# Seven-product hidden layer: a ScalarE copy from PSUM bank to PSUM bank that later products add onto, and ScalarE copies where VectorE added

## The chip, the cores and the metric

The kernel runs on one core of a Trainium2 chip. The engines are named as in the profile: PE is TensorE's matmul and PEld its weight load, DVE is VectorE, ACT is ScalarE, POOL is GpSimd, SP is the engine that issues most DMAs. PE writes its results to PSUM banks (128 partitions x 512 float32), and DVE and ACT read them from there. The metric is the device time of one execution in microseconds, as the median of several runs; lower is better.

## The reference

Two blocks follow each other, all in float32. `x` is (8, 8, 512, 64): batch, head, token, depth; `state` is (8, 8, 32, 64).

```python
scores  = scale * x @ state^T;   a  = softmax(scores);   xread = a @ state
scores2 = scale * state @ x^T;   a2 = softmax(scores2);  sread = a2 @ x
t = concatenate([xread, sread], axis=2)        # (8, 8, 544, 64)
t = t.transpose(0, 2, 1, 3).reshape(8 * 544, 512)
h = t @ w_in                                   # (4352, 2048)
g = h * erf(softplus(h))
out = g @ w_out                                # (4352, 512)
```

## The kernel before

Each batch gives 512 token rows and 32 state rows. Batch 0 runs through a start of its own, whose order of steps is written out in a long string. Batches 1 to 7 run through one loop with two **rounds** per batch, 14 in all; a round makes one half of the 2048 hidden columns for the 512 token rows of its batch. The state rows of all batches come last (`hidden_states`, `project7`).

A round calls `hidden_wide`. The product of the attention weights `aT` (512 tokens) and the mixed weights `m` is cut into 2 x 2 blocks, and the four blocks c11, c12, c21, c22 of the hidden layer are made with seven block products in place of eight (the Winograd form of Strassen's scheme). The sums of blocks that go in stand in `sx` and `sy`, made earlier on DVE by `combine_m` and `combine_a`. `hidden_wide` goes through two **halves** (`o` = 0 and 1), and each half makes the seven products for two blocks of 128 hidden columns, so there are 28 halves. `product(n, bank, first)` is two matmuls of float32, which PE runs in two passes each: four passes and four weight loads of L489. With `first` false the product is added onto what the bank holds.

A half of before uses two banks of `ps_h` (tile `h`), then two of `ps_at` (tile `at`); both pools have two buffers. The scheme's sums are taken so: with P1 to P7 the products,

- product 1 goes to bank p, ACT copies it to `m1` in SBUF (L495);
- product 6 goes to bank q, DVE makes u2 = m1 + P6 (L499 by way of L472);
- product 2 is added onto P1 in p, ACT copies c11 (L504);
- product 7 is added onto P6 in q, DVE makes u3 = m1 + P6 + P7 (L508);
- product 5 in a new bank, DVE makes c22 = u3 + P5 (L514); product 4 in another, DVE makes c21 = u3 + P4 (L517);
- product 3 is added onto P5, DVE makes c12 = u2 + P5 + P3 (L522).

All five adds go through the helper `add`, so the profile puts them at L472. u2 and u3 lie in the places of c12 and c21 in the SBUF tile `ring`. ACT takes Softplus of each block (L482), in the order 0, 3, 2, 1; the last one of a half (`late`) is emitted in the next half, or at the end. The first Softplus of a round stands behind an ACT table load.

Between the products stand two kinds of other work. `between()` takes one **piece** of the projection of the round before (`project_wide`, two matmuls of L641; in the first round one 512 wide matmul of L926), with the copies and adds that follow from it (L646, L664 on ACT, L626 on DVE; in the first round the copy L932 on ACT). `fill(budget)` takes DVE steps from a list: softmax steps of the next batch, transposes, `combine_m`, differences of `w_out`. Instructions on PE, DVE and ACT run in the order in which they are emitted:

```python
in_order(begun, [nc.tensor, nc.vector, nc.scalar])
```

After `hidden_wide` a round takes erf on ACT, multiplies by the hidden block on DVE (L1127), makes sums of blocks (L673, L674), and projects with seven products again (`project_wide`), during which attention scores, `mixed_pair` (L383 to L386) and reads for the next batches are woven in.

Of the kernel before, what the change touches and what calls it, by code (L numbers as in the profile page):

```python
# [9 lines left out]
F32 = mybir.dt.float32  # L10
# [7 lines left out]
def kernel(  # L18
# [17 lines left out]
    nc = tc.nc  # L36
    B, H, S, D = x.shape
    Ns = state.shape[2]
    d_model, d_ff = moe_w_in.shape
    P = 128  # L40
# [19 lines left out]
    ps_at = ctx.enter_context(tc.tile_pool(name="ps_at", bufs=2, space=PSUM))  # L60
# [408 lines left out]
    def hidden_wide(b, g, low, between, fill, later):  # L469

        bank = lambda: ps_h.tile([P, S], F32, name="h")
        add = lambda o, x, y: nc.vector.tensor_tensor(o, x, y, op=ALU.add)  # L472
        view = lambda t: t.rearrange("p (h u) -> p h u", h=2)
        late = None
        for o in range(2):
            s, hs = ([ring[:, u, low:low + 2, k, 2 * o:2 * o + 2].rearrange(
                "p h i t -> p h (i t)") for k in range(4)] for u in range(2))
            c11, c12, c21, c22 = hs
            m1, u2, u3 = s[3], c12, c21

            def softplus(k, s=s, hs=hs):
                nc.scalar.activation(out=s[k], in_=hs[k], func=ACTF.Softplus)  # L482

            def product(n, bank, first=True):
                x, y = X[b, g][n - 1], Ys[b][n - 1]
                out = bank.rearrange("p (h i t) -> p i h t", h=2, i=2)
                for i in range(2):
                    q = P * (2 * o + i)
                    nc.tensor.matmul(out=out[:, i], lhsT=x[:, q:q + P], rhs=y,  # L489
                                     start=(first and i == 0), stop=(i == 1),  # L490
                                     skip_group_check=not first)

            p, q = bank(), bank()
            product(1, p)
            nc.scalar.copy(m1, view(p))  # L495
            if late:
                late(1)
            product(6, q)
            add(u2, m1, view(q))  # L499
            if o or not later:  # L500
                between()
            fill(1.8)
            product(2, p, False)
            nc.scalar.copy(c11, view(p))  # L504
            if not o and later:
                between()
            product(7, q, False)
            add(u3, m1, view(q))  # L508
            softplus(0)
            between()  # L510
            fill(1.2)
            p, q = (ps_at.tile([P, S], F32, name="at") for _ in range(2))
            product(5, p)
            add(c22, u3, view(p))  # L514
            product(4, q)
            softplus(3)
            add(c21, u3, view(q))  # L517
            between()
            fill(0.6 if o else 1.2)
            product(3, p, False)  # L520
            softplus(2)
            add(c12, u2, view(p))  # L522
            fill(0 if o else 1.2)
            late = softplus
        late(1)
# [551 lines left out]
    for n, name in enumerate(steps0):  # L1077
        if n == len(steps0) - 40:
            overlap = traced()
        n, _, name = name.rpartition("*")  # L1080
# [17 lines left out]
    def fill(budget):  # L1098
        while jobs and jobs[0][0] <= budget + 0.01:
            cost, f = jobs.popleft()  # L1100
            budget -= cost
            f()
# [32 lines left out]
    for n, (b, u) in enumerate((b, u) for b in range(1, B) for u in range(2)):  # L1135
# [42 lines left out]

        steps = pending()
        hidden_wide(b, o, low, lambda: next(steps, None), fill, n == 0)  # L1180
        erf_part(inner, outside)
        for k, _ in enumerate(steps):
# [141 lines left out]
```

## Time and profile before

| | before |
|---|---|
| time, median of 3 runs | 716.93 us (716.89 to 716.95) |
| profiled execution, span from first to last instruction | 716.0 us |
| PE busy, TensorE matmul instructions in the trace | 709.2 us (99%), 4291 |
| DVE busy | 541.9 us (76%), 880 instructions |
| ACT busy | 378.9 us (53%), 535 instructions |
| DVE adds of L472, from `at` and from `h` | 84 x 680 ns, 56 x 679 ns |
| ACT copies L495 and L504 | 28 x 585 ns, 28 x 586 ns |
| ACT Softplus L482 and its table loads | 112 x 631 ns, 14 x 1283 ns |

The span runs from the first to the last instruction of one profiled execution; the device time of a run also has what lies around it. Busy times of the engines overlap. PE's ends are modelled, so that a busy PE may still have short gaps; the distance between the starts of its passes or of its weight loads is the better measure. "Idle before" and the name behind the arrow say how long an engine stood before an instruction and what released it.

### The profile page before, as it was taken

What the parts mean: (1) busy time and instruction counts of PE and PEld (TensorE: products, weight loads), DVE (VectorE), ACT (ScalarE), POOL (GpSimd) and SP (SyncE); (2) the same over time, 40 slices, a digit from 0 to 9 for tenths busy, and PEclk for the clock granted to TensorE, in tenths of its full rate; (3) what the DMA queues carried; (4) which work ended last, traced back from release to release, by engine and by line L of the source; (5) the groups of instructions that cost most, each with busy time, mean ns of one, the idle gap of its engine ahead of it and who ended that gap; (6) DMA issues with size and microseconds to landing.
All of it is one profiled execution on the core that took longest, in us unless ns stands there. A gap on an engine that the chain in (4) does not pass through costs nothing.

```text
span 716.0 us, 10962 instructions
## 1 busy us (share of the span) xinstructions
PE 709.2 (99%) x4291; PEld 562.4 (79%) x4291; DVE 541.9 (76%) x880; ACT 378.9 (53%) x535; POOL 25.2 (4%) x34
## 2 busy tenths in 40 slices
PE   8999999999999999999999999999999999999998
PEld 6444347688878878887888878887888888889997
DVE  6997888889868987698776877697777757665533
ACT  4999895647364526544455445562464535442340
POOL 0000000000100000000000000000000000000000
PEclk9999999999999999999999999999999999999999
DMA  8779686750358162514523280615242322002100
GB/s 257 236 209 251 210 243 180 169 159 31 52 98 205 28 140 40 161 37 106 80 41 138 58 148 1 177 31 144 34 120 70 95 41 27 33 29 30 25 7 30
DMA packets 144068, 74.65 MB, mean 104 GB/s; under 512 B 123024, under 2 KB 132624, under 8 KB 142480
## 3 DMA queue, kind: packets, MB, share of 16 engines
q1 hardware_dynamic: 139152, 65.89, 33.8%
q0 software_dynamic: 4032, 7.34, 7.6%
q8 instruction: 34, 0.56, 0.3%
q10 hardware_dynamic: 832, 0.72, 0.3%
q14 instruction: 18, 0.15, 0.1%
HBM read 49.81 MB, written 20.45 MB: 98 GB/s over the span
## 4 chain that ended last, share of the span: by engine, by line
PE 97%; DMA 2%; ACT 0%; SPq 0%; DVE 0%; issue 0%
PE o L641 48%; PE h L489 14%; PE at L489 10%; PE o L926 8%; PE h L534 3%; PE o L616 3%; PE at L919 2%; PE h L919 2%; PE h L383 2%; DMA raw<-in_moe_w_out_dram 2%; PE at L383 2%; PE at L275 1%; PE o L224 1%; DMA x<-in_x_dram 1%; PE at L908 1%; PE at L1018 0%
## 5 line engine op out<-in xcount | busy, mean ns | idle before, releaser
L641 PE MATMUL o<-w_out,ring 128*128 128x256 f32 x896 | 203.0, 379 | 0.0
L641 PEld LDWEIGHTS o<-w_out,ring 128*128 128x128 f32 x896 | 169.8, 190 | 24.9 <-DVE ring L1127 0.8
L641 PE MATMUL o<-raw,ring 128*128 128x256 f32 x672 | 161.4, 381 | 0.0
L641 PEld LDWEIGHTS o<-raw,ring 128*128 128x128 f32 x672 | 126.5, 190 | 25.9 <-ACT m L385 9.2
L482 ACT ACTIVATE ring<-ring 128x512 f32<-128x512 f32 x112 | 70.6, 631 | 59.8 <-DVE ring L472 59.2
L489 PE MATMUL h<-aT,m 128*128 128x256 f32 x336 | 81.9, 379 | 0.0
L1127 DVE TENSOR_TENSOR ring<-ring 128x1024 f32<-128x1024 f32 (+1 forms) x61 | 70.7, 1201 | 4.5 <-ACT ring L546 4.5
L489 PEld LDWEIGHTS h<-aT,m 128*128 128x128 f32 x336 | 63.8, 190 | 10.2 <-issue 0.9
L472 DVE TENSOR_TENSOR ring<-ring,at 128x512 f32<-128x512 f32 x84 | 57.2, 680 | 16.9 <-PE at L489 15.2
L926 PE MATMUL o<-w_out,ring 128*128 128x512 f32 x128 | 59.5, 599 | 0.0
L626 DVE TENSOR_TENSOR ot<-uv,o 128x256 f32<-128x256 f32 (+1 forms) x56 | 31.0, 553 | 30.1 <-PE o L641 28.1
L472 DVE TENSOR_TENSOR ring<-ring,h 128x512 f32<-128x512 f32 x56 | 38.0, 679 | 20.0 <-PE h L489 19.9
L664 ACT COPY ot<-o 128x256 f32<-128x256 f32 x28 | 10.4, 372 | 77.9 <-PE o L641 77.9
L704 POOL DMA_DIRECT2D out_dram<-ot x28 | 24.5, 946 | 652.1 <-DVE ot L626 574.8
L926 PEld LDWEIGHTS o<-w_out,ring 128*128 128x128 f32 x128 | 23.7, 190 | 28.1 <-issue 26.6
L626 DVE TENSOR_TENSOR ot<-ot,o 128x256 f32<-128x256 f32 x56 | 22.2, 417 | 27.9 <-ACT ot L664 27.7
L504 ACT COPY ring<-h 128x512 f32<-128x512 f32 x28 | 16.4, 586 | 47.9 <-PE h L489 47.9
L673 DVE TENSOR_TENSOR ring<-ring 128x512 f32<-128x512 f32 x56 | 38.6, 689 | 1.4
L674 DVE TENSOR_TENSOR ring<-ring 128x512 f32<-128x512 f32 x56 | 36.3, 685 | 0.0
L385 ACT COPY m<-h 128x512 f32<-128x512 f32 x13 | 7.6, 586 | 46.7 <-PE h L383 46.6
L546 ACT ACTIVATE ring<-ring 128x2048 f32<-128x2048 f32 x16 | 30.5, 1904 | 0.0
L489 PE MATMUL at<-sy,sx 128*128 128x256 f32 x112 | 28.7, 379 | 0.0
(203 smaller groups left out, 965.8 us busy)
## 6 DMA issues: line engine op xcount, KB each, us to landing
w_in<-kept_in SPq DMA_DIRECT2D x7, 2048.0 KB, 8.2
out_dram<-ot SPq DMA_DIRECT2D x33, 256.0 KB, 2.2
raw<-in_moe_w_in_dram SPq DMA_DIRECT2D x16, 512.0 KB, 5.4
raw<-in_moe_w_out_dram SPq DMA_DIRECT2D x8, 1024.0 KB, 5.9
xq<-in_x_dram SPq DMA_DIRECT2D x112, 64.0 KB, 3.2
x<-in_x_dram SPq DMA_DIRECT2D x56, 128.0 KB, 3.0
out_dram<-ot POOLq DMA_DIRECT2D x28, 256.0 KB, 4.5
sc<-xT SPq DMA_DIRECT2D x112, 32.0 KB, 1.9
```

What stands on the lines that cost most here:

```text
L383: nc.tensor.matmul(out=ps[k][e][q, :], lhsT=st[r, b, q], rhs=of_group[g][r, :, i, :], start=True, stop=True)
L472: add = lambda o, x, y: nc.vector.tensor_tensor(o, x, y, op=ALU.add)
L482: nc.scalar.activation(out=s[k], in_=hs[k], func=ACTF.Softplus)
L489: nc.tensor.matmul(out=out[:, i], lhsT=x[:, q:q + P], rhs=y, start=(first and i == 0), stop=(i == 1), skip_group_check=not first)
L546: nc.scalar.activation(out=s, in_=s, func=ACTF.Erf)
L626: add = lambda o, x, y: tt(o, x, y, op=ALU.add)
L641: nc.tensor.matmul(out=out, lhsT=lhs[:, i, :], rhs=rhs[:, g, i, :], start=(start and i == 0), stop=(i == GF - 1), skip_group_check=not start)
L673: return [lambda: tt(S1, A21, A22, op=ALU.add), lambda: tt(S2, S1, A11, op=ALU.subtract), lambda: tt(S3, A11, A21, op=ALU.subtract), lambd ...
L674: lambda: tt(S3, A11, A21, op=ALU.subtract), lambda: tt(S4, A12, S2, op=ALU.subtract)]
L919: nc.tensor.matmul(out=h_t[g, i], lhsT=m_t[0, g][:, e, P * i:P * i + P], rhs=aT[0][:, e], start=start, stop=not start)
L926: nc.tensor.matmul(out=acc[r], lhsT=gT[g][:, i, P * r:P * r + P], rhs=w_out[:, GF * g + i, :], start=(made_of[r] == 1), stop=(made_of[r] = ...
L1127: nc.vector.tensor_tensor(s[:, ks], s[:, ks], hs[:, ks], op=ALU.mult)
```

## The change

In each half, ACT no longer copies product 1 to `m1` in SBUF; it copies the whole bank p into the second bank q. Product 5 moves up to stand right behind product 1, in a bank r of `ps_at`. Products 6, 7 and 4 are then all added onto the contents of q, one after the other, and after each of them ACT copies the bank out: u2, u3 and c21. The DVE adds that made u2, u3 and c21 are gone; c22 = u3 + r and c12 = u2 + r stay on DVE, and product 3 is added onto product 5 in r. A half allocates three banks in place of four. `m1` is no longer used here. The pieces, the `fill` calls and the Softplus calls stay where they were among products 6, 2, 7, 4 and 3.

```diff
-            m1, u2, u3 = s[3], c12, c21
+            u2, u3 = c12, c21
...
             p, q = bank(), bank()
+            r = ps_at.tile([P, S], F32, name="at")
             product(1, p)
-            nc.scalar.copy(m1, view(p))
+            nc.scalar.copy(q, p)
             if late:
                 late(1)
-            product(6, q)
-            add(u2, m1, view(q))
+            product(5, r)
+            product(6, q, False)
+            nc.scalar.copy(u2, view(q))
             if o or not later:
                 between()
             fill(1.8)
...
             if not o and later:
                 between()
             product(7, q, False)
-            add(u3, m1, view(q))
+            nc.scalar.copy(u3, view(q))
+            add(c22, u3, view(r))
             softplus(0)
             between()
             fill(1.2)
-            p, q = (ps_at.tile([P, S], F32, name="at") for _ in range(2))
-            product(5, p)
-            add(c22, u3, view(p))
-            product(4, q)
+            product(4, q, False)
             softplus(3)
-            add(c21, u3, view(q))
+            nc.scalar.copy(c21, view(q))
             between()
             fill(0.6 if o else 1.2)
-            product(3, p, False)
+            product(3, r, False)
             softplus(2)
-            add(c12, u2, view(p))
+            add(c12, u2, view(r))
             fill(0 if o else 1.2)
             late = softplus
         late(1)
```

In the changed kernel the ACT copies have the lines L496 (bank to bank), L501 (u2), L506 (c11), L510 (u3) and L517 (c21).

## The prediction

> **What bounds the kernel now.** I read the page first: busy time by engine, and the chain of work that ended last.
>
> ```profile
> PE 709.2 (99%) x4291; PEld 562.4 (79%) x4291; DVE 541.9 (76%) x880; ACT 378.9 (53%) x535; POOL 25.2 (4%) x34
> PE 97%; DMA 2%; ACT 0%; SPq 0%; DVE 0%; issue 0%
> ```
>
> TensorE is busy all the time and is 97% of the chain. DVE and ACT appear there with 0%: taking work off DVE pays only where PE waits for DVE, and putting work on ACT costs only where PE comes to wait for ACT. The fourteen rounds (calls of `hidden_wide`, two halves each) that the change touches lie between 107 and 633 us. Second view, busy time by stage (after the stage: its length, PE busy, PEld busy, DVE, ACT), and third, what the weight loads waited for in that stage (total, times, longest).
>
> ```profile
> 100.00:640.00 540.00, 540.00 (x3248) 448.24 (x3247) 423.30 (x707) 274.61 (x407) 21.08 (x24) 1.00 0.39 90
> PEld h L489 <- DVE ring L472: 0.3, 1, 0.3
> PEld h L489 <- ACT ring L495: 0.3, 1, 0.3
> ```
>
> PE is busy for all 540 us at clock 1.00, and of 784 weight loads of L489 one waited for a DVE add (L472) and one for the ACT copy (L495). So the DVE adds cost no time now. The fourth view is the order of time in one round (start, duration; x4 means four weight loads, one product), weight loads first, then ACT:
>
> ```profile
> 459.64 0.84 PEld L489 LDWEIGHTS h<-aT,m 128*128 128x128 f32 x4
> 460.50 0.84 PEld L489 LDWEIGHTS h<-sy,sx 128*128 128x128 f32 x4
> 461.36 0.84 PEld L641 LDWEIGHTS o<-w_out,ring 128*128 128x128 f32 x4
> ...
> 468.27 0.84 PEld L489 LDWEIGHTS h<-aT,m 128*128 128x128 f32 x4
> 460.92 0.59 ACT L495 COPY ring<-h 128x512 f32<-128x512 f32 x1 [0.49 <-PE h L489]
> 463.51 0.59 ACT L504 COPY ring<-h 128x512 f32<-128x512 f32 x1 [2.00 <-PE h L489]
> 464.11 1.28 ACT L482 ACT_TABLE_LOAD   x1
> 465.41 0.63 ACT L482 ACTIVATE ring<-ring 128x512 f32<-128x512 f32 x1
> 465.94 0.35 ACT L646 COPY uv<-o 128x256 f32<-128x256 f32 x1
> 469.55 0.59 ACT L495 COPY ring<-h 128x512 f32<-128x512 f32 x1 [1.16 <-PE h L489]
> 472.14 0.59 ACT L504 COPY ring<-h 128x512 f32<-128x512 f32 x1 [1.47 <-PE h L489]
> 472.76 0.63 ACT L482 ACTIVATE ring<-ring 128x512 f32<-128x512 f32 x1
> ```
>
> From 459.64 to 468.27 there are ten groups (seven products, three pieces of the projection), so a group takes 0.863 us and its four PE passes 0.216 each. An ACT copy of a product starts 0.42 after the next group's first weight load (460.50 to 460.92, 469.13 to 469.55).
>
> The fifth view is the one place where PE did wait for such a copy, the first half of the first round (second column: duration):
>
> ```profile
> 108.24 0.84 PEld L489 LDWEIGHTS h<-sy,sx 128*128 128x128 f32 x4
> 108.46 1.03 PE L489 MATMUL h<-sy,sx 128*128 128x256 f32 x4
> 108.72 0.57 ACT L495 COPY ring<-h 128x512 f32<-128x512 f32 x1
> 109.34 0.51 PEld L489 LDWEIGHTS h<-aT,m 128*128 128x128 f32 x3 [0.25 <-ACT ring L495]
> 110.31 1.02 PE L926 MATMUL o<-w_out,ring 128*128 128x512 f32 x2
> ```
>
> The copy ends at 109.29, the weight load starts 0.05 later, and that is 0.24 after its turn (108.24 + 0.863 = 109.10). But PE itself lost only 0.125: from 108.46 to 110.31 are 1.85 us for eight passes that take 1.725. The weight load runs ahead of its pass, and this lead hides 0.11 of a late start.
>
> **The change, part by part.** The order of the built kernel on PE is now, per half (28 of them): product 1, 5, 6, piece, 2, 7, piece, 4, piece, 3. In the very first half the first piece stands behind product 2.
>
> *What goes.* The m1 copy (L495, 585 ns) becomes the copy from bank to bank, so 28 for 28. Three of five DVE adds per half go: 84 x 0.68 = 57 us of DVE. On the path this is worth nothing, by the third view.
>
> *What comes on ACT.* Three copies of 586 ns per half, 84 x 0.586 = 49 us. A half has 5.45 us of ACT work (five copies, four Softplus) in 8.63; it fits as a mean, and what counts are the waits.
>
> *Wait 1, product 6 for the bank copy.* Only product 5 lies between product 1 and product 6: 0.863 us of cover. Needed are 0.42 + 0.586 + 0.05 = 1.056. The weight load is 0.193 late, the lead hides 0.11, PE loses 0.083. No row of before shows ACT writing into a bank. Bounds: Softplus (SBUF to SBUF) takes 631 ns, reads of a bank 586 to 597; so 631 above, which makes the loss 0.128; below, the saving on the other side too, or more, until at 503 ns nothing is lost. I take 586, the nearest row, which has one of the two ends in a bank. The Trainium skill (ScalarE: Activation LUTs, "Step-by-step: what each stage is for") says that ScalarE writes faster to PSUM than to SBUF, without a figure; no run here shows it, and by it the term would lie between 0 and 0.083. The skill also speaks against the whole edit (PSUM — Partial Sum Buffer, "Summary: rules for kernel authors"): a seed that ACT writes has to be 0, because whether the next matmul adds to it hangs on bits that ACT does not set; no row here shows such bits, and time would be the same either way.
>
> *Wait 2, product 4 for the u3 copy.* Before, product 4 had a fresh bank. Now it adds onto the bank that u3 is copied from, one group after product 7: again 0.863 of cover against 1.056, and this copy has the form of L504. PE loses 0.083.
>
> *Waits that are covered.* Product 7 waits for the u2 copy, which ends 1.87 after product 6 begins; product 7 begins 2.59 after, so 0.7 is to spare (also behind the late Softplus that the second half puts in between). Product 2 is behind product 6 and finds the copy done. Product 3 waits for c22 = u3 + r: 0.03 + 0.68 + 0.05 after the u3 copy, 2.63 after product 7 begins, against 3.54. DVE now stands still at c22 until the u3 copy is there; queued behind are the softmax, transpose and sx steps of `fill`, and c12. With three adds less per half they come no later than now, and their readers are a stage away.
>
> *ACT's queue in front of the second bank copy.* In the first half of a round the table load now stands behind the u3 copy, and behind it, in order: Softplus 0, L646, Softplus 3, the c21 copy, Softplus 2, and then the bank copy of the second half. From the end of the u3 copy, by the starts above: 0.01 + 1.30 (load) + 0.53 + 0.25 (L646 less its overlap) + 0.53 + 0.62 (a Softplus that needs the copy in front, 472.14 to 472.76) + 0.53 = 3.77. The u3 copy ends 1.87 after product 7 begins, so ACT is free at 5.64; product 1 of the second half begins at 5 x 0.863 + 0.083 = 4.40 and can be copied at 5.68. It just fits, with 0.04 to spare. In the first round L932 (604 ns) stands there in place of L646, some 0.25 longer: 0.2 us lost once. The skill (same page, "What ACT_TABLE_LOAD costs") counts 2.66 us for a table switch, load and drain. Here the Softplus starts 1.30 after the load does, so the row has no drain; by the page the bank copy would be 1.34 late in 14 rounds and the sum 18 us higher.
>
> *Sum.* Two waits in 28 halves are 56; one (fifth view) is paid already. 55 x 0.083 = 4.6, and 0.2 makes 4.8. PE has nothing to make it up with. The profiled execution has a span of 716.0 and the median is 716.93, 0.9 for what lies around it: 716.9 + 4.8 = 721.7.
>
> **Rivals.** *A, ACT's queue becomes the bound.* If the seven steps in front of the second bank copy take 0.3 longer than I add up (c22 late from DVE holds Softplus 3 and all behind it), each round loses 0.3 and more: 14 x 0.3 = 4 on top, 726 and beyond. For it: 0.04 of slack. Against: c22 has 1.3 us before Softplus 3 needs it, and DVE has less to do.
> *B, not slower: the lead of the weight load hides both waits.* Place: the first weight loads of products 6 and 4; price 0.083 each; it decides from a lead of 0.19 on. Time 717.0. For it: the lead of 0.11 is from one wait only. Against: that wait was just such a copy.
> *C, faster.* DVE with 57 us less feeds something earlier. The most there is to win in this stage is PE's gap at changes of shape, well under 5 us, and the waits put to DVE are parts of a microsecond: 716.
>
> **How the numbers follow.** Forecast 0.82, A 0.09, B 0.06, C 0.03. Below, a bank copy of 503 ns or less leaves 4.8 - 2.3 = 2.5, 719.4; above, 631 ns adds 28 x 0.045 = 1.3, and a queue 0.15 late in 13 rounds 2.0: 725.0. The range is 719.2 to 725.0; it leaves out A's worse half and B and C. What a measurement can tell from no change is 0.2%, 1.4 us; the forecast is slower in all its range, as is A: 0.91. B is the same: 0.06; C faster: 0.03.
>
> **What would show it.** After: the weight loads of L489 wait for L496 and for L510 some 28 times each, about 0.2 each; ten groups take 8.80 in place of 8.63; L496 takes 586 ns give or take 45; ACT is busy some 428 us, DVE some 485; PE still leads the chain. The forecast is wrong if those waits are absent (B), if L496 starts more than 0.1 after ACT could have had product 1 in second halves (A), or if PE's weight loads come to wait for DVE's c22 at product 3.

## The result, and the profile after

The changed kernel takes 722.12 us (median, 721.6 to 722.54) against 716.94 for the kernel before; the ratio is 1.0068, 95% interval 1.0054 to 1.0083. Both were run again beside each other on the chip of the last experiments: 722.44 against 717.72, 4.7 us apart, ratio 1.0065 (1.0052 to 1.0077). In all runs of the experiments the kernel before lies near 717.7 with spans near 716.0, so 1.8 us lie outside the span there, where the first table had 0.9. Times below are compared within one chip.

The page of the profiled execution after (722.54 us, span 720.8), busy time and chain:

```profile
PE 714.0 (99%) x4291; PEld 558.4 (77%) x4291; DVE 489.0 (68%) x796; ACT 420.9 (58%) x619; POOL 25.2 (3%) x34
PE 97%; DMA 2%; ACT 0%; issue 0%; SPq 0%; DVE 0%
```

DVE has 53 us less and ACT 42 us more, and the same PE work takes 5 us longer. The chain still puts all of it down to PE. What PE lost shows in the waits of its weight loads between 100 and 645 us (total, times, longest):

```profile
PEld h L489 <- ACT ring L510: 6.8, 28, 0.6
PEld h L489 <- ACT h L496: 6.0, 28, 0.3
```

Two waits per half, 28 times each: product 4 for the u3 copy, product 6 for the copy from bank to bank. In order of time, the weight loads of a half that answers to the one shown of before, then ACT up to the second bank copy:

```profile
462.44 0.84 PEld L489 LDWEIGHTS h<-aT,m 128*128 128x128 f32 x4
463.30 0.84 PEld L489 LDWEIGHTS at<-sy,sx 128*128 128x128 f32 x4
464.39 0.73 PEld L489 LDWEIGHTS h<-sy,sx 128*128 128x128 f32 x4 [0.25 <-ACT h L496]
465.15 0.84 PEld L641 LDWEIGHTS o<-w_out,ring 128*128 128x128 f32 x4
...
467.74 0.84 PEld L641 LDWEIGHTS o<-w_out,ring 128*128 128x128 f32 x4
468.79 0.73 PEld L489 LDWEIGHTS h<-sy,m 128*128 128x128 f32 x4 [0.21 <-ACT ring L510]
469.54 0.84 PEld L641 LDWEIGHTS o<-raw,ring 128*128 128x128 f32 x4
...
471.27 0.84 PEld L489 LDWEIGHTS h<-aT,m 128*128 128x128 f32 x4
463.77 0.57 ACT L496 COPY h<-h 128x512 f32<-128x512 f32 x1 [0.55 <-PE h L489]
468.15 0.58 ACT L510 COPY ring<-h 128x512 f32<-128x512 f32 x1 [0.28 <-PE h L489]
468.75 1.28 ACT L482 ACT_TABLE_LOAD   x1
470.05 0.63 ACT L482 ACTIVATE ring<-ring 128x512 f32<-128x512 f32 x1
470.58 0.35 ACT L646 COPY uv<-o 128x256 f32<-128x256 f32 x1
470.84 0.63 ACT L482 ACTIVATE ring<-ring 128x512 f32<-128x512 f32 x1
471.37 0.57 ACT L517 COPY ring<-h 128x512 f32<-128x512 f32 x1
471.97 0.63 ACT L482 ACTIVATE ring<-ring 128x512 f32<-128x512 f32 x1
472.55 0.57 ACT L496 COPY h<-h 128x512 f32<-128x512 f32 x1
```

Product 6's weight load starts 0.05 after the bank copy's end (463.77 + 0.57 = 464.34, 464.39), 0.23 after its turn; product 4's 0.06 after L510's end, 0.19 after its turn. The half takes 8.83 us (462.44 to 471.27) where it took 8.63. Taking each distance between the starts of PE's passes less what the pass takes without a stall (0.216 us for 256 columns, 0.429 for 512), products 6 lost 2.30 us in all and products 4 2.23: 4.53, against 0.12 before.

### The profile page after: what moved, and what is told of

The parts are those of the page before. It is cut to its first block, busy times and chain, and to the rows that moved or that the text cites. A ratio compares the mean times of both kernels' runs of the same rounds, so it can differ in the third digit from the quotient of the medians.

```text
span 720.8 us, 10926 instructions
## 1 busy us (share of the span) xinstructions
PE 714.0 (99%) x4291; PEld 558.4 (77%) x4291; DVE 489.0 (68%) x796; ACT 420.9 (58%) x619; POOL 25.2 (3%) x34
## 4 chain that ended last, share of the span: by engine, by line
PE 97%; DMA 2%; ACT 0%; issue 0%; SPq 0%; DVE 0%
PE o L641 47%; PE h L489 17%; PE o L926 8%; PE at L489 7%; PE h L534 3%; PE o L616 3%; PE at L919 2%; PE h L919 2%; PE h L383 2%; DMA raw<-in_moe_w_out_dram 2%; PE at L383 2%; PE at L275 1%; PE o L224 1%; PE at L908 1%; DMA x<-in_x_dram 1%; PE at L1018 0%
## 5 line engine op out<-in xcount | busy, mean ns | idle before, releaser
L472 DVE TENSOR_TENSOR ring<-ring,at 128x512 f32<-128x512 f32 x56 | 38.2, 682 | 86.6 <-ACT ring L510 79.5
L489 PE MATMUL h<-aT,m 128*128 128x256 f32 x336 | 81.8, 379 | 0.0
L489 PEld LDWEIGHTS h<-aT,m 128*128 128x128 f32 x336 | 63.8, 190 | 10.0 <-issue 1.2
L626 DVE TENSOR_TENSOR ot<-uv,o 128x256 f32<-128x256 f32 (+1 forms) x56 | 31.0, 553 | 37.7 <-PE o L641 35.9
L626 DVE TENSOR_TENSOR ot<-ot,o 128x256 f32<-128x256 f32 x56 | 22.1, 416 | 27.8 <-ACT ot L664 27.7
L506 ACT COPY ring<-h 128x512 f32<-128x512 f32 x28 | 16.4, 585 | 29.6 <-PE h L489 29.6
L501 ACT COPY ring<-h 128x512 f32<-128x512 f32 x28 | 16.4, 586 | 28.0 <-PE h L489 25.5
L489 PE MATMUL h<-sy,m 128*128 128x256 f32 x112 | 31.0, 399 | 0.0
L489 PE MATMUL h<-sy,sx 128*128 128x256 f32 x112 | 30.9, 398 | 0.0
```

Source lines behind the costliest of these rows:

```text
L489: nc.tensor.matmul(out=out[:, i], lhsT=x[:, q:q + P], rhs=y, start=(first and i == 0), stop=(i == 1), skip_group_check=not first)
L626: add = lambda o, x, y: tt(o, x, y, op=ALU.add)
```

## The experiments

Every kernel below was timed beside the kernel before on its chip (717.68, 717.76 and 717.72 in the three sets of runs), and times are compared by their distance to it; the change stands 4.7 above. "PE's loss" is the sum just described, for the products of L489 unless another line is named. "Cover" below is the PE work that lies between a product and the next one that needs its bank. All of them:

| run | time | ratio to before (95%) | PE's loss: product 6 / product 4 / elsewhere |
|---|---|---|---|
| the change, again | 722.44 | 1.0052 to 1.0077 | 2.29 / 2.25 / - |
| third piece before product 4 | 721.40 | 1.0042 to 1.0067 | 3.22 / 0 / - |
| first piece before product 6 | 723.89 | 1.0075 to 1.0106 | 0.13 / 2.25 / product 7: 3.55 |
| product 5 late | 744.29 | 1.0357 to 1.0386 | 26.4 / 0 / - |
| u3 copied by VectorE | 727.26 | 1.0121 to 1.0149 | 2.23 / 7.17 / - |
| product 4 in its own bank | 720.50 | 1.0029 to 1.0054 | 2.99 / 0 / - |
| both waits covered | 720.61 | 1.0029 to 1.0054 | 0.13 / 0 / projection: 2.3 more |
| the same, c22 behind fill | 717.63 | 0.9992 to 1.001 | 0.13 / 0 / - |
| order alone, c22 behind fill | 722.48 | 1.0053 to 1.0081 | 0 / 0 / product 3: 5.55 |
| order alone, c22 first | 717.29 | 0.9987 to 1.0005 | 0 / 0 / - |
| third piece before 4, Softplus 2 later | 721.09 | 1.0036 to 1.0061 | 3.00 / 0 / - |

**Is the change's cost the same on one chip?**

> The changed kernel as it is, beside the kernel before on the same chip. The traces put the stalls at 4.3 us; the kernel before took 717.7 in the runs of the experiments, 0.8 more than in the first table, all of it outside the span. Theory: 717.7 + 4.4 = 722.1 on one chip. Rival (something outside the stalls adds 0.8): 722.9.

Measured: 722.44 against 717.72. The spans are 720.7 and 716.0, so all 4.7 us lie inside them. 4.4 are the stalls (4.54 less the 0.12 of before). Some 0.3 us more lie behind PE's last pass (3.98 us from its start to the end, 3.65 in the traces of before and of the covered kernel); why is open.

**Product 5 late: the law of the wait, with nothing between.**

```diff
             product(1, p)
             nc.scalar.copy(q, p)
-            product(5, r)
             product(6, q, False)
...
             between()
             fill(1.2)
+            product(5, r)
+            add(c22, u3, view(r))
             product(4, q, False)
```

> Product 5 stands behind the second piece again, in front of product 4, so nothing lies between product 1 and product 6, and product 4 has two groups of cover. Theory: product 6 waits 0.42 + 0.571 + 0.05 - 0.11 = 0.93 us each time, 28 x 0.93 = 26.0, in place of 2.1; the wait of product 4 goes, -2.2: 722.1 + 23.9 - 2.2 = 743.8. Rival (added ScalarE work): unchanged, 722.

Measured: 744.29, and the waits of product 6 alone rise to the foreseen size:

```profile
PEld h L489 <- ACT h L496: 30.2, 28, 1.1
```

ScalarE does the same work as in the change. What changed is 0.863 us of cover per half, and PE lost 26.4 us where 26.0 were worked out; product 4, with two groups of cover now, lost nothing. The rival that ScalarE's added work is the cost falls here.

**u3 copied by VectorE: a lighter ScalarE, a slower kernel.**

```diff
-            nc.scalar.copy(u3, view(q))
+            nc.vector.tensor_copy(u3, view(q))
```

> The copy of u3 goes from ScalarE to VectorE, nothing else. Theory: what counts is how long the copy keeps the bank. VectorE starts 0.49 us after the next group's first weight load and its operations on 128x512 take about 0.68: 0.49 + 0.68 + 0.05 - 0.863 - 0.11 = 0.25 in place of 0.08 at product 4, 28 x 0.17 = 4.7 more: 726.8. Rival (added ScalarE work): ScalarE has 16 us less, the loss shrinks by about a third, 720.4. Second rival (VectorE standing still at c22 until ScalarE has copied u3 costs time): gone here, faster than 722.1.

Measured: 727.26, 9.5 above before, so 4.8 more than the change (4.7 foreseen). The group of the copy (28 x 692 ns) and the wait:

```profile
L510 DVE COPY ring<-h 128x512 f32<-128x512 f32 x28 | 19.4, 692 | 64.1 <-PE h L489 62.2 <-issue 1.8
PEld h L489 <- DVE ring L510: 11.8, 28, 0.8
```

ScalarE had 16 us less to do and PE lost 4.9 us more. What counts is how long the copy keeps the bank: 692 ns and a start 0.485 us after product 7's last pass begins, against 585 ns and 0.416. Both rivals fall.

**Undoing one wait, in two ways.** First by cover, then by a bank of its own:

```diff
+            between()
             product(4, q, False)
             softplus(3)
             nc.scalar.copy(c21, view(q))
-            between()
```

> The third piece of the projection stands in front of product 4 in place of behind it, so the u3 copy has two groups of cover (1.73 us) in place of one. Theory (each bank that ACT copies has to be free before the next product, and only what the cover leaves open costs): the wait of product 4 for L510 goes, 28 x 0.080 = 2.2 us, 722.1 becomes 719.9; the wait of product 6 for L496 stays at 0.08 each. Rival (ScalarE's 42 us of added work is what slows the kernel): that work is unchanged, so 722.1.

```diff
-            r = ps_at.tile([P, S], F32, name="at")
+            r, r4 = (ps_at.tile([P, S], F32, name="at") for _ in range(2))
+            if o:
+                r, r4 = r4, r
...
-            product(4, q, False)
+            product(4, r4)
             softplus(3)
-            nc.scalar.copy(c21, view(q))
+            add(c21, u3, view(r4))
```

> Of the changed kernel only product 4 is undone: it goes into a bank of its own and VectorE adds c21 = u3 + that bank. Theory: product 4 no longer waits for L510, 2.2 us won, 719.9, as with the third piece moved in front of it; the wait of product 6 stays. Rival (added ScalarE work): 16 of 42 us gone, 720.4, which a time alone does not tell from the theory; the weight loads' waits do.

Measured: 721.40 and 720.50. In both the wait for L510 is gone, 2.25 us of PE's loss. But the wait for the bank copy (L496, in the second run L498) grew:

```profile
PEld h L489 <- ACT h L496: 7.0, 28, 0.5
PEld h L489 <- ACT h L498: 6.7, 28, 0.3
```

PE's loss there went from 2.29 to 3.22 and 2.99, which I had not foreseen; so the first stands 3.7 above before and the second 2.7, where 2.5 was expected of both (4.7 less 2.2). The rest of the two distances, some 0.3 more and 0.4 less, is behind PE's last pass (4.26 and 3.65 us from its start to the end, 3.98 in the change). ACT's queue in the first of the two, at the second half's bank copy:

```profile
193.55 0.63 ACT L482 ACTIVATE ring<-ring 128x512 f32<-128x512 f32 x1
194.09 0.58 ACT L496 COPY h<-h 128x512 f32<-128x512 f32 x1
```

No idle time stands before L496: it follows Softplus 2 at once, 0.046 later than PE's result would have let it (1.33 after product 1's first weight load in place of 1.28). The 0.04 us to spare that the prediction had counted are used up, because product 1 now comes 0.08 earlier and the table load does not. In the first round the copy is 0.27 late. The next run tests this.

**Softplus 2 moved out of that queue.** In addition to the third piece before product 4:

```diff
             if late:
+                late(2)
                 late(1)
...
-            softplus(2)
+            if o:
+                softplus(2)
```

> The third piece in front of product 4, as in the first run, and of a first half the Softplus 2 moved behind the bank copy of the second half. Theory: the first run took away the wait of product 4 but the wait of product 6 grew from 2.2 to 2.9 us, because ScalarE's queue (table load and all behind it) has only 0.04 us to spare in front of the second bank copy and product 1 came 0.08 earlier. With 0.6 us less in that queue the growth goes: 721.4 becomes 720.7, and L496 starts 1.28 after product 1 begins in second halves. Rival (a wait of another kind): stays at 721.4.

Measured: 721.09, and product 6 lost 3.00, not the 2.3 that it loses in the change. A miss, and an instructive one:

```profile
194.09 0.57 ACT L496 COPY h<-h 128x512 f32<-128x512 f32 x1 [0.58 <-PE h L489]
```

ScalarE now stood idle for 0.58 us before the copy, so the queue no longer holds it. Yet the copy ends as late after the pass as it did: it starts 0.471 us after product 1's last pass begins and takes 570 ns, where in the first run it started after 0.461 and took 579. With no Softplus in between that waits for the c21 copy, the bank copy itself has to wait for two semaphores, PE's and ScalarE's own (the c21 copy has to have left the bank). An extra semaphore instruction then stands in front of it on ACT's queue; of L496, first in the run before, then in this one:

```profile
L496 ACTq EVENT_SEMAPHORE  x12: 17/17/862, 107.2 to 581.4; - x12
L496 ACTq EVENT_SEMAPHORE  x26: 17/17/861, 107.4 to 627.4; - x26
```

Where this extra instruction is the one that waits for PE, the copy starts 0.471 after the pass; copies with one semaphore start 0.416 after it. Where it waits for a DVE result that has long been there, as in four first halves of the change, the copy starts 0.416 after the pass all the same. The 0.471 shows in the change itself, in six of its first halves, in the run with product 4's own bank (second halves) and, below, at L503. What this run did win of PE's loss, 0.22 us, is in the first round, where the second bank copy now starts 0.471 after the pass and not 0.685.

**More cover for product 6: the wait moves.**

```diff
             product(5, r)
+            if o or not later:
+                between()
             product(6, q, False)
             nc.scalar.copy(u2, view(q))
-            if o or not later:
-                between()
```

> The first piece stands in front of product 6 in place of behind it (not in the very first half). Theory: the bank copy is covered now, 28 x 0.08 = 2.1 us won, but between products 6 and 7 only product 2 is left, 0.863 us against the 1.05 that the u2 copy needs: the same wait comes back at product 7 for L501, 0.08 each. Time 722.1, and the weight loads wait for L501 in place of L496. Rival (the bank to bank copy is what is slow): 720.0.

Measured: 723.89, 6.2 above before, 1.5 more than the change.

```profile
PEld h L489 <- ACT ring L503: 7.2, 27, 0.3
PEld h L489 <- ACT ring L510: 6.9, 28, 0.6
```

The wait left L496 and came back at product 7 for the u2 copy (L503), as foreseen. It is larger, 3.55 in 27 halves or 0.13 each, since L503 waits for two semaphores and starts 0.46 to 0.47 after the pass. The rival, that the copy into a bank is the slow thing, falls.

**Both waits covered, with the copies kept on ScalarE.**

```diff
             product(5, r)
+            if o or not later:
+                between()
             product(6, q, False)
             nc.scalar.copy(u2, view(q))
-            if o or not later:
-                between()
...
             product(2, p, False)
             nc.scalar.copy(c11, view(p))
-            if not o and later:
-                between()
+            between()
             product(7, q, False)
             nc.scalar.copy(u3, view(q))
             add(c22, u3, view(r))
             softplus(0)
-            between()
+            if not o and later:
+                between()
             fill(1.2)
-            product(4, q, False)
+            product(4, r4)
             softplus(3)
-            nc.scalar.copy(c21, view(q))
+            add(c21, u3, view(r4))
```

> Product 4 goes into a bank of its own again and c21 is a VectorE add again; the first piece stands in front of product 6 and the second in front of product 7 (not in the very first half). The bank copy and the copies of u2 and u3 stay on ScalarE. Order of a half: 1, 5, piece, 6, 2, piece, 7, 4, piece, 3. Theory: every wait has two groups of cover, so all 4.4 us of stalls go: 717 to 718, the time of before. Rival (added ScalarE work): a third of the 42 us is gone, so a third of the loss, 720.4.

Measured: 720.61, a miss. All waits of L489 for ScalarE's copies are gone (but the one of the very first half), and a new one came in the projection (L628 is the projection's add, L626 before):

```profile
PEld o L643 <- DVE uv L628: 3.0, 5, 0.6
```

The cause was looked for on VectorE, in the order of time of that kernel:

```profile
191.63 0.69 DVE L472 TENSOR_TENSOR ring<-ring,at 128x512 f32<-128x512 f32 x1 [4.05 <-ACT ring L511]
```

VectorE stands still for 4.05 us at c22, until ScalarE has copied u3, which is a group later in this order; the `fill` steps queued behind come late, and with them the projection's add. The next run moves c22 behind them and nothing else. (`r4` is a bank of its own for product 4, made as above.)

```diff
             nc.scalar.copy(u3, view(q))
-            add(c22, u3, view(r))
             softplus(0)
...
             fill(1.2)
+            add(c22, u3, view(r))
             product(4, r4)
```

> The kernel in which both waits have two groups of cover (product 4 in its own bank, c21 on VectorE, pieces in front of 6 and 7) lost its ScalarE waits but lost 0.34 us in eight rounds at the projection's add of L628 instead. Here c22 is emitted behind the fill steps, not in front of them, nothing else. Theory: VectorE stood at c22 until ScalarE had copied u3 (some 7.1 us into a half) and came late to all that was queued behind; with the fill steps in front it works in that time, the projection's waits go, 2.3 to 2.9 us, and the time is that of before on the same chip, 717.7. Rival (the bank copies on ScalarE cost something beside the waits): stays at 720.6.

Measured: 717.63, ratio 1.0001 (0.9992 to 1.001): the time of before. The five waits for L628 are gone (five in the trace, not the eight rounds of the expectation). The stay at c22 is shorter now, with work in front of it:

```profile
190.59 1.48 DVE L472 TENSOR_TENSOR ring<-ring,at 128x512 f32<-128x512 f32 x2 [2.72 <-ACT ring L511]
```

This kernel's page shows what the added work on ScalarE and the relief of VectorE are worth when no wait is left over:

```profile
PE 709.0 (99%) x4291; PEld 561.7 (78%) x4291; DVE 507.3 (71%) x824; ACT 407.9 (57%) x591; POOL 25.2 (4%) x34
```

29 us more on ACT and 35 less on DVE than before, with the copy from bank to bank kept, change the time neither way.

**The order of the products alone.** The kernel before with product 5 moved up and nothing else; c22 once behind the `fill` steps, once right behind u3.

> The kernel before with product 5 moved up behind product 1, as in the change; m1, the three VectorE adds and four banks stay as before. Theory: the order alone costs nothing, 716.9. Rival (the new order of the products, and c22 placed earlier on VectorE, costs something): up to 722.

Measured: 722.48, which at first sight spoke for the rival. But the wait named its own cause:

```profile
PEld at L489 <- DVE ring L472: 9.1, 20, 0.8
```

In my edit c22 had stayed behind the `fill` steps, and with product 5 in front product 7 comes one group later, so that product 3 found its bank not yet read. Hence the second run:

> The kernel before with only product 5 moved up (all five VectorE adds, m1 and four banks as before), and c22 right behind u3 on VectorE as in the change, where the run before it had c22 behind the fill steps and product 3 waited for it, 5.5 us in all. Theory: that wait was the place of c22; product 3 finds its bank free, and the time falls from 722.5 to 717.7 or, if VectorE with its full load then comes late to the steps behind, to 718 to 720. Rival (the new order itself costs): stays near 722.5.

Measured: 717.29, ratio 0.9996 (0.9987 to 1.0005). The order is free. Placing c22 behind `fill` is a loss with five adds on VectorE and a gain with three: the same line, judged by what stands idle.

No version beat the kernel before beyond the noise. The trace of before has PE busy for all of 540 us in these rounds. By the starts of its passes the projection, the largest part of that, loses 1.5 us in 15 gaps of 0.10; what the smaller parts lose was not worked out.

## Why the prediction was right

The forecast was 721.7, in a range of 719.2 to 725.0; measured 722.1. Term by term:

- *The mechanism* is as forecast: the copy keeps the bank longer than one group covers. Undone alone, doubled in cover, lengthened (VectorE) and left bare (product 5 late) the waits answered by the sum 0.42 + copy + 0.05 - cover - 0.11, within 0.5 us over 28 halves; what it left out is the second semaphore, 0.04 to 0.055 where it counts.
- *Wait 1* was put at 0.083; it is 0.063 in most halves, 0.118 in the six whose copy starts 0.471 after the pass, 0.082 on the mean. That the mean came out is luck: a copy that is 15 ns shorter than assumed and a second semaphore that was not foreseen cancel. The copy into a bank takes 571 ns, not 586. The Trainium skill (ScalarE: Activation LUTs, "Step-by-step: what each stage is for") has ScalarE faster towards PSUM; here that is 14 ns against the same copy into SBUF (L510, 585 ns).
- *Wait 2* was put at 0.083; it is 0.080.
- *The lead of 0.11*, read from one wait, held: from it 0.93 and 0.25 were worked out for two of the experiments, and 0.94 and 0.26 came.
- *ACT's queue* was put at 3.77 us and its slack at 0.04. In the trace shown, the u3 copy ends at 468.73 and Softplus 2 starts at 471.97; a copy behind a Softplus can start 0.54 after it (193.55 to 194.09 above), so ScalarE was free 3.78 after the u3 copy, and the bank copy started 0.04 later. Rival A was as close as that, and the third piece before product 4 tipped it.
- *The first round* was put at 0.2 for L932; PE lost 0.06 there, since the copy started 0.04 late and took 595 ns. This term was mis-sized: it puts L932 in the place of L646, in front of Softplus 3, but the trace has it behind the c21 copy:

```profile
116.45 0.57 ACT L517 COPY ring<-h 128x512 f32<-128x512 f32 x1
116.91 0.59 ACT L932 COPY ot<-o 128x512 f32<-128x512 f32 x1
117.39 0.64 ACT L482 ACTIVATE ring<-ring 128x512 f32<-128x512 f32 x1
117.92 0.59 ACT L496 COPY h<-h 128x512 f32<-128x512 f32 x1
```

  There it fills part of the time in which Softplus 2 waits for the c21 copy. From L517 to Softplus 2 are 0.94 us, where the round shown above takes 0.60 (471.37 to 471.97): 0.34 longer, of which L646 had taken 0.26 in its own place (470.58 to 470.84). With the third piece in front of product 4, L932 does stand in front of Softplus 3, and the copy is the 0.27 late named above.
- *The table load*: 468.75 to 470.05 is 1.30 again, as in the row of before. The Trainium skill (ScalarE: Activation LUTs, "What ACT_TABLE_LOAD costs") counts 2.66 with a drain; no run here shows a drain behind these loads.
- *DVE's relief is worth nothing*: shown by the covered kernel. *DVE standing at c22* was called harmless, which is right for the change (L626's waits did not grow) but has little room: one group later it cost 2.3 us.
- *The other signs* came: the half shown takes 8.83 us against 8.80. ACT is busy 420.9 us against 428 and DVE 489.0 against 485, because the page counts overlapping instructions once; their durations added up grew by 48.5 us on ACT and fell by 57.4 on DVE, as forecast.

The sum of 4.8 stands against 4.7 on one chip. Of these 4.4 are the two waits (4.6 in the forecast). That the rest agrees too is luck: most of the 0.2 for L932 did not come, and 0.3 behind PE's last pass, which no term of the forecast has, came in its place. Why it came is open.

## What to carry to other kernels

When PE is the bound, moving work between two engines with idle time can be free (here 29 us onto ScalarE and 35 off VectorE), as long as no result comes late for it. What cost here is a bank handed from PE to another engine and back: count from the last pass to the copy's start, the copy, and the release, and compare with the PE work that lies between. Here that chain is 1.04 to 1.1 us and one product of 0.86 does not cover it; two do, or a bank of its own. In an in-order queue an instruction that waits for a slower engine belongs behind the steps that are ready, as long as its own reader can wait.

## What the runs showed of the hardware that was not expected

- An ACT copy whose waits are on two semaphores takes an extra semaphore instruction. Where that instruction waits for the PE pass, the copy starts 0.471 us after the start of the pass, against 0.416 with one semaphore; where it waits for something long done, the copy starts at 0.416 too.
- A copy of 128x512 float32 from bank to bank takes ScalarE 571 ns, into SBUF 585 to 586; on VectorE the latter takes 692.
- A weight load that is late by 0.17 to 0.24 us costs PE 0.06 to 0.13; late by 0.36 (u3 on VectorE) it costs 0.26, and by 1.04 (product 5 late) 0.93. The difference is 0.11 each time, behind passes of 256 columns.
